# Attention and maxout layers fused on one core: the second key batch's q moved behind its phi, k and v, with a new hand order of all pieces

## The chip, the cores and the metric

The kernel runs on one core of one Trainium2 chip. The metric is the device time of one execution in microseconds (us). Before the change the median of three runs is 160.75 us (160.62 to 160.98).

## The reference

Eight batches, eight heads, 576 positions, head size 64, 32 memory slots. All inputs and the output are float32.

```python
# q, k, v: (8, 8, 576, 64); phi: (8, 8, 576, 32)
a = softmax(phi, axis=2)                        # over the positions
k_m = einsum('bhsm,bhsd->bhmd', a, k)
v_m = einsum('bhsm,bhsd->bhmd', a, v)
attn = softmax(q @ k_m.T / 8, axis=-1) @ v_m    # (8, 8, 576, 64)
x = attn.transpose(0, 2, 1, 3).reshape(4608, 512)
h = maximum(maximum(x @ w1, x @ w2), x @ w3)    # w: (512, 768)
out = h @ w_out                                 # (768, 512)
```

## The kernel before

Everything is cut into pieces, one letter each, and one long string of words writes the order out by hand: `B@2` is piece B of batch 2, a number behind the letter is a part of it, and a `!` (the argument `swap`) gives a part of the piece's work to the other of two engines. `issue` (L769) turns a word into a call. Each engine runs its own instructions strictly in the order of the words, and waits at the first one whose inputs or buffers aren't ready. A second string, `banks`, gives the PSUM bank of each accumulation, in the same order.

What a batch goes through, with the letters:

- **Loads**, issued from GpSimd's queue: `L0` phi, `L1` k, `L2` v, `L3` q (L93, L97, L97, L112); `J0` and `J1` are the two halves of q of batch 1. k, v and q are converted from float32 to bf16 by the DMA, phi stays float32. phi and q have two buffers each, k two, and the tile that holds packed k beside v (`kvr`) three. `Y` loads weights. These DMAs share one queue and land in the order of their issue.
- **Sums over positions**: `E` exponentiates phi on ScalarE. From batch 2 on, `r` copies k into `kvr` (on GpSimd, with `!` on ScalarE, L102), so that `B` (L247) gives the sums of k and v and the softmax denominator in one pass. Batches 0 and 1 do it in two: `B0` for k, `B1` for v. `N` (L269) divides by the denominator: a reciprocal on VectorE, and then the scaling, one instruction for v and two for k on VectorE, or with `!` two and two on ScalarE. `K` (L309) transposes the result and copies it out of PSUM (VectorE, with `!` ScalarE).
- **Scores**: `Q0`, `Q1` transpose q in blocks on VectorE (L323); `S` (L337) multiplies and exponentiates on ScalarE. `a`, `s`, `c`, `m`, `X` form the softmax of the scores on VectorE (`m` without `!` on GpSimd). `M`, `R`, `X` do it another way, with ScalarE, for three groups of batches 0 and 1.
- **Folded weights**: `D` multiplies v_m into the weights w1 - w3 and w2 - w3 (`D3`: into w3 times w_out), casts by ScalarE or VectorE. `V0` to `V3` (L213) subtract w3 from columns 0 to 511, 512 to 767, 1024 to 1535 and 768 to 1023 of w1 and w2, on VectorE or, with `!`, GpSimd. They overwrite the weights that the folds of batch 0 have read, and come before the folds of batch 1.
- **First layer**: `F0` to `F11` (L505), even ones followed by a relu on ScalarE (with `!` VectorE), odd ones by a maximum on VectorE.
- **Second layer**: for batches 0 and 1 `t` (L667) does the first four of six blocks and `T` (L680) the rest, or `T` does all; `g` sends a row block of batch 0 by ScalarE's queue. From batch 2 on it is done by a Strassen-like scheme of seven products `P` (L590), with sums `A` of activations and sums `U` of weights, on GpSimd or VectorE. `U0` to `U3` with @9 are the sums of w_out.

PSUM has eight banks; `B`, `D`, `F` and each half of `S` take two, the others one. A piece waits until the previous user of its banks has been copied out.

Of the kernel before, what the change touches and what calls it, by code (L numbers as in the profile page):

```python
# [15 lines left out]
def kernel(  # L16
# [14 lines left out]
    B, H, S, D = q.shape  # L31
# [32 lines left out]
    K1 = NP * NC * KS  # L64
# [73 lines left out]
    for i in range(P // M):  # L138
# [4 lines left out]
    banks = iter(  # L143
        "".join(
            """
            00232204420145545045026406426402640264023462467420742602462062460264024603604206
            42604620642164646240624607402604260240402402420724062042642024204204260424026427
            402742002442072420426045026520026265260602406243352
            """.split()
        )  # L150
    )
# [658 lines left out]
    for w in """  # L810
        E@0 h2@0 h3@0 h0@0 h1@0 L3@0 Z25@0 B0@0 Y2@0 I@0 N0@0 Z2@0 K0@0! Q0@0 Q1@0 Z9@0 S@0 Z2@0
        M0@0 M1@0 R0@0 R1@0 W0@0 Y3@0 W1@0 W2@0 Z6@0 O1@0 H3@0 O3@0 O2@0 H1@0 X1@0 B1@0
        X0@0 N1@0 K1@0 O0@0 Y0@0 D1@0! D0@0! D3@0 F10@0 F0@0! F8@0 Y1@0 L0@1 L1@1 J0@1
        F2@0! F6@0 V0@0! D4@0! D2@0 E@1 J1@1 F4@0! F1@0 F5@0 L2@1 F3@0 F7@0 F9@0 L3@2
        F11@0 B0@1 N0@1! t1@0 L1@2 t2@0 Q1@1 Q0@1 T2@0 K0@1! V1@0 V3@0 T1@0 S@1 L0@2
        B1@1 U0@9! N1@1! M1@1 a0@1 R1@1 t3@0 K1@1! T3@0 L2@2 s0@1 L1@3 c0@1 V2@0 D0@1
        D1@1! L0@3 D2@1 L2@3 t0@0 r0@2 X1@1 m0@1! X0@1 T0@0 F10@1! Q0@2 F6@1 E@2 F7@1
        F0@1 g2@0 F11@1 L3@3 F1@1 D3@1 Q1@2 F2@1 B@2 U1@9 F4@1 L1@4 L0@4 N@2 F3@1 F8@1
        K@2 g1@0 F5@1 L2@4 S@2 F9@1 D1@2! t3@1 E@3 D0@2 D2@2 D3@2 L3@4 a@2 T3@1 s@2 U3@9
        T4@1! c@2 m@2! r0@3 X@2 B@3 F0@2 U0@2 N@3 F8@2! F6@2 K@3 U1@2 Q0@3 L1@5 F2@2  # L820
        L0@5 Q1@3 U3@2 F10@2 g0@0 F3@2 F4@2 F9@2 F11@2 U2@9 S@3 a@3 s@3 t2@1 c@3 g3@0
        D3@3 D2@3 L2@5 U2@2 D0@3 U0@3 t0@1 r0@4! E@4 F1@2 T0@1! U1@3 F5@2 T2@1! F7@2
        t1@1 m@3 L3@5 A0@2! X@3 L0@6 T1@1! F6@3 F4@3! D1@3! B@4 N@4 L1@6 A1@2! F0@3 Q1@4
        F2@3 Q0@4 L2@6 A2@2! F8@3 K@4! F7@3 P1@2! F1@3 S@4 P2@2 F10@3 D0@4 a@4 D1@4!
        P0@2 A3@2! s@4 c@4 F3@3 P4@2 E@5 r0@5! F11@3 F9@3 m@4 F5@3 L3@6 P5@2 A0@3! T4@3!
        A1@3! D3@4 B@5 X@4 N@5 D2@4 Q1@5 Q0@5 P6@2 F2@4 K@5 P3@2 F10@4! S@5 L1@7 P1@3!
        D2@5 D1@5! a@5 F11@4 P2@3 F8@4 s@5 c@5 U2@3 L0@7 F4@4! F0@4 F6@4 r0@6! L2@7 P0@3
        F1@4 F7@4 F9@4 P4@3 E@6 A2@3! A3@3! F3@4 F5@4 P3@3 D0@5 m@5 L3@7 U3@3 D3@5 B@6
        A0@4! A1@4! X@5 N@6 P5@3 F6@5 F8@5! Q0@6 r0@7 F2@5 Q1@6 F10@5 K@6! F9@5 U0@5
        F4@5 F7@5 P6@3! S@6 E@7 F3@5 P1@4 a@6 F5@5 F11@5 P2@4 D0@6 U0@4 B@7 D3@6 U2@4  # L830
        N@7 s@6 P0@4 A2@4! F0@5 F1@5 Q1@7 K@7! U1@4 A3@4! P4@4 D1@6! A0@5! D1@7! c@6
        D2@7! m@6 P3@4! U3@4 P5@4! D0@7 D2@6 D3@7 U2@6 Q0@7 X@6 T4@5 S@7 A1@5! A3@5!
        P6@4! F10@6 a@7 F6@6 s@7 F4@6 F11@6 F0@6 F7@6 c@7 P1@5 P2@5 F2@6! U2@5 F5@6 F3@6
        P0@5 U1@5 F1@6 m@7 F8@6 A2@5! X@7 P4@5 P3@5 F4@7 U0@6 U1@6 F10@7 U3@5 F9@6 P5@5!
        F5@7 F8@7 A0@6! P1@6! A1@6! F2@7 F6@7 F0@7 P6@5! U0@7 F7@7 F3@7 F1@7 P2@6! F11@7
        F9@7 A0@7 P0@6 A2@6! A1@7 P4@6 A3@6 U3@6! P1@7 P2@7 A2@7 P5@6 P3@6 U2@7! U1@7
        P4@7 P0@7! A3@7 P6@6 U3@7! P5@7 P3@7! P6@7! T4@7!
    """.split():
        n, b = w.rstrip("!").split("@")
        issue(int(b), n, w.endswith("!"))  # L840
# [30 lines left out]
```

## Time and profile before

| | |
|---|---|
| median of three runs | 160.75 us (160.62 to 160.98) |
| the profiled execution | 160.76 us, of which the span of the profile is 159.0 us |
| granted TensorE clock | 0.999 of full speed |
| busy | TensorE 149.6 us (94%), VectorE 116.8, GpSimd 109.2, ScalarE 98.8 |
| moved by DMA | 31.78 MB, 200 GB/s on average |

The profiled execution lies 0.01 us from the median of the runs, so a sum that is made against its trace can be read against the median as it is; 1.76 us of it are outside the span. "Idle before" an instruction means that its engine stood still; a releaser is what it waited for. Most of the 42 warm-up matmuls of line 164 (11.8 us) fill the first 20 us, in which little has been loaded.

In the issue table, the time to landing of a load counts from its issue on GpSimd to the moment that its completion can be seen.

### The profile page before, as it was taken

What the parts mean: (1) busy time and instruction counts of PE and PEld (TensorE: products, weight loads), DVE (VectorE), ACT (ScalarE), POOL (GpSimd) and SP (SyncE); (2) the same over time, 40 slices, a digit from 0 to 9 for tenths busy, and PEclk for the clock granted to TensorE, in tenths of its full rate; (3) what the DMA queues carried; (4) which work ended last, traced back from release to release, by engine and by line L of the source; (5) the groups of instructions that cost most, each with busy time, mean ns of one, the idle gap of its engine ahead of it and who ended that gap; (6) DMA issues with size and microseconds to landing.
All of it is one profiled execution on the core that took longest, in us unless ns stands there. A gap on an engine that the chain in (4) does not pass through costs nothing.

```text
span 159.0 us, 5179 instructions
## 1 busy us (share of the span) xinstructions
PE 149.6 (94%) x2218; PEld 100.3 (63%) x2228; DVE 116.8 (73%) x203; ACT 98.8 (62%) x142; POOL 109.2 (69%) x101
## 2 busy tenths in 40 slices
PE   6987798999798999999999999999999999999992
PEld 2442443574456538556776768887774888888871
DVE  2022803698988899787989688999998895679871
ACT  3205335723888699799699878886788826424110
POOL 7961102995039948889999999799969997890000
PEclk9999999999999999999999999999999999999999
DMA  5999999999999999999999999999303500332554
GB/s 150 168 199 209 205 210 211 281 207 210 207 281 225 298 236 243 307 262 214 323 246 277 213 255 284 278 239 246 111 0 136 200 4 0 132 132 70 177 187 164
DMA packets 22934, 31.78 MB, mean 200 GB/s; under 512 B 1152, under 2 KB 18560, under 8 KB 22912
## 3 DMA queue, kind: packets, MB, share of 16 engines
q0 software_dynamic: 16128, 21.43, 70.2%
q1 hardware_dynamic: 6064, 8.85, 15.8%
q10 hardware_dynamic: 720, 1.18, 2.2%
q8 instruction: 17, 0.28, 0.7%
q14 instruction: 5, 0.04, 0.1%
HBM read 39.32 MB, written 9.44 MB: 307 GB/s over the span
## 4 chain that ended last, share of the span: by engine, by line
PE 72%; DMA 19%; POOL 5%; issue 1%; ACT 1%; POOLq 0%
PE psum L513 26%; PE psum L624 24%; DMA w_sb<-in_moe_w_dram 13%; DMA kvr<-in_v_dram 6%; PE psum L462 5%; PE psum L690 4%; PE psum L672 3%; PE psum L256 3%; PE psum L699 2%; PE psum L351 2%; POOL ko L97 1%; PE psum L708 1%; POOL qq L112 1%; POOL w_sb L119 1%; PE psum L753 1%
## 5 line engine op out<-in xcount | busy, mean ns | idle before, releaser
L513 PE MATMUL psum<-hx,wp 128*128 128x288 bf16 x384 | 53.7, 286 | 0.7 <-DVE wp L181 0.3
L513 PEld LDWEIGHTS <-wp 128*128 128x128 bf16 x384 | 36.6, 98 | 12.3 <-issue 1.5
L526 DVE TENSOR_TENSOR hx<-psum,h 128x576 bf16<-128x576 f32 x48 | 34.1, 744 | 3.3 <-PE psum L513 2.7
L177 ACT CAST wp<-psum 128x1024 bf16<-128x1024 f32 (+1 forms) x30 | 28.2, 993 | 2.7 <-PE psum L462 2.3
L175 ACT ACTIVATE h<-psum 128x576 bf16<-128x576 f32 x38 | 23.8, 651 | 8.9 <-PE psum L513 8.7
L624 PEld LDWEIGHTS <-hx 128*128 128x128 bf16 x192 | 18.4, 98 | 3.5 <-issue 0.9
L360 ACT ACTIVATE e<-psum 128x576 bf16<-128x576 f32 x16 | 9.5, 649 | 7.5 <-PE psum L351 7.5
L549 POOL TENSOR_TENSOR w_sb<-hx 128x1024 bf16<-128x1024 bf16 x5 | 10.6, 2130 | 4.0 <-DVE hx L526 2.6
L164 PE MATMUL psum<-warm 128*128 128x512 bf16 x42 | 11.8, 435 | 1.4 <-DVE warm L131 1.2
L330 DVE STREAM_TRANSPOSE qT<-qq 128x576 f32<-128x576 f32 x16 | 11.6, 757 | 2.0 <-DMA qq<-in_q_dram 2.0
L624 PEld LDWEIGHTS <-w_sb 128*128 128x128 bf16 x120 | 11.4, 98 | 2.5 <-issue 0.7
L107 POOL COPY kvr<-ko 128x2304 bf16<-128x2304 bf16 x3 | 6.3, 2108 | 7.7 <-DMA ko<-in_k_dram 7.7
L218 POOL TENSOR_TENSOR w_sb<-w_sb 128x2048 bf16<-128x2048 bf16 x1 | 4.1, 4065 | 10.4 <-PE psum L462 10.4
L436 POOL TENSOR_TENSOR t<-t,sm 128x1152 bf16<-128x1152 bf16 x5 | 10.6, 2127 | 0.6 <-DVE sm L429 0.5
L549 POOL TENSOR_TENSOR w_sb<-w_sb,hx 128x1024 bf16<-128x1024 bf16 x5 | 10.6, 2128 | 0.3
L234 ACT ACTIVATE e<-ph 128x1152 bf16<-128x1152 f32 (+1 forms) x9 | 9.6, 1063 | 1.8 <-DMA ph<-in_phi_dram 1.8
L549 POOL TENSOR_TENSOR hx<-hx 128x1024 bf16<-128x1024 bf16 x5 | 10.7, 2130 | 0.0
L549 POOL TENSOR_TENSOR twb<-wp 128x256 bf16<-128x256 bf16 x11 | 7.3, 670 | 3.9 <-ACT wp L177 3.9
L624 PE MATMUL psum<-w3T,hx 128*128 128x256 bf16 x72 | 9.8, 273 | 0.0
L624 PE MATMUL psum<-wo_sb,hx 128*128 128x256 bf16 x72 | 9.8, 273 | 0.0
L656 DVE TENSOR_TENSOR ot<-psum,snap 128x512 f32<-128x512 f32 x12 | 8.3, 689 | 1.9 <-PE psum L624 1.3
L97 POOL DMA_DIRECT2D ko<-in_k_dram x11 | 7.7, 700 | 2.9 <-DMA qq<-in_q_dram 1.5
(106 smaller groups left out, 272.2 us busy)
## 6 DMA issues: line engine op xcount, KB each, us to landing
out_dram<-ot SPq DMA_DIRECT2D x8, 512.0 KB, 4.2
qq<-in_q_dram POOLq DMA_DIRECT2D x7, 576.0 KB, 13.5
ph<-in_phi_dram POOLq DMA_DIRECT2D x7, 576.0 KB, 15.3
ko<-in_k_dram POOLq DMA_DIRECT2D x7, 576.0 KB, 16.1
kvr<-in_v_dram POOLq DMA_DIRECT2D x7, 576.0 KB, 18.0
out_dram<-ot SPq DMA_DIRECT2D x14, 256.0 KB, 2.2
w_sb<-in_moe_w_dram POOLq DMA_DIRECT2D x3, 768.0 KB, 17.9
out_dram<-ot ACTq DMA_DIRECT2D x4, 256.0 KB, 6.2
```

The costliest lines, as they stand in the source:

```text
L97: nc.gpsimd.dma_start(out=kv[:, h].rearrange("p j c d -> p j (c d)"), in_=by_pair((k, v)[i], b)[:, h],)
L164: nc.tensor.matmul(po[:, 0:BANK], lhsT=warm[:, 0:P], rhs=warm, start=True, stop=True)
L175: nc.scalar.activation(out=out_, in_=in_, func=AF.Relu)
L177: nc.scalar.copy(out=out_, in_=in_)
L234: nc.scalar.activation(out=s["e"][:, js], in_=loaded[b]["ph"][:, js], func=AF.Exp)
L330: nc.vector.transpose(out=s["qT"][:, j].rearrange("p j c r e -> p (j c r e)").bitcast(FP32), in_=loaded[b]["q"][:, j].rearrange("p j c d - ...
L360: nc.scalar.activation(out=e2[:, a].rearrange("p (t r c) -> p t r c", t=2, c=NC), in_=sc[a][:, :, 0:SH].rearrange("p t (c r) -> p t r c", ...
L436: (nc.vector if swap else nc.gpsimd).tensor_tensor(out=t, in0=t, in1=x.to_broadcast(list(t.shape)), op=ALU.mult,)
L513: nc.tensor.matmul(acc[:, h, 0:SH], lhsT=wps[b][:, g, w * DF + ft * P : w * DF + (ft + 1) * P], rhs=attn[:, g, c0 : c0 + SH], start=(g == ...
L526: nc.vector.tensor_tensor(out=hT[:, row(ft), (b % 2) * S : (b % 2 + 1) * S].rearrange("p (h n) -> p h n", h=2), in0=a, in1=s["h1", ft], op ...
L549: eng.tensor_tensor(out=out_, in0=in0, in1=in1, op=op)
L624: nc.tensor.matmul(po[:, q * CH : (q + 1) * CH], lhsT=lhs(k, q), rhs=rhs(k), start=(i < 3 and k == 0 and q == 0), stop=(k == KT and q == 1 ...
```

## The change

No piece is added or dropped: the same 382 words behind the common start stand in another order, some with `!` put on or taken off, and with other PSUM banks.

- q of batch 2 (`L3@2`) is issued behind phi, k and v of batch 2; before it came ahead of them. The order becomes phi, k, v, q.
- `r0@2` (the packing of k of batch 2 on GpSimd) now comes ahead of the four loads of batch 3.
- The block `t0@0` moves ahead of `B0@1`; `S@1` comes ahead of `T1@0`.
- Of the weight differences, `V1@0` goes to GpSimd and `V0@0` to VectorE (before the other way round), and `U0@9` goes from VectorE to GpSimd.
- `N` of batches 2 and 7 scales on ScalarE (batch 1 did already). `K` of batches 2 and 3 is copied out by ScalarE.
- Behind batch 3, order and engines of many first-layer and second-layer pieces differ. The last three words are the same.

```diff
     banks = iter(
...
-            00232204420145545045026406426402640264023462467420742602462062460264024603604206
...
+            00232204420145545045026402640240624602467406065460260246042064064204620465026406
...
-        X0@0 N1@0 K1@0 O0@0 Y0@0 D1@0! D0@0! D3@0 F10@0 F0@0! F8@0 Y1@0 L0@1 L1@1 J0@1
-        F2@0! F6@0 V0@0! D4@0! D2@0 E@1 J1@1 F4@0! F1@0 F5@0 L2@1 F3@0 F7@0 F9@0 L3@2
-        F11@0 B0@1 N0@1! t1@0 L1@2 t2@0 Q1@1 Q0@1 T2@0 K0@1! V1@0 V3@0 T1@0 S@1 L0@2
-        B1@1 U0@9! N1@1! M1@1 a0@1 R1@1 t3@0 K1@1! T3@0 L2@2 s0@1 L1@3 c0@1 V2@0 D0@1
-        D1@1! L0@3 D2@1 L2@3 t0@0 r0@2 X1@1 m0@1! X0@1 T0@0 F10@1! Q0@2 F6@1 E@2 F7@1
-        F0@1 g2@0 F11@1 L3@3 F1@1 D3@1 Q1@2 F2@1 B@2 U1@9 F4@1 L1@4 L0@4 N@2 F3@1 F8@1
-        K@2 g1@0 F5@1 L2@4 S@2 F9@1 D1@2! t3@1 E@3 D0@2 D2@2 D3@2 L3@4 a@2 T3@1 s@2 U3@9
-        T4@1! c@2 m@2! r0@3 X@2 B@3 F0@2 U0@2 N@3 F8@2! F6@2 K@3 U1@2 Q0@3 L1@5 F2@2
-        L0@5 Q1@3 U3@2 F10@2 g0@0 F3@2 F4@2 F9@2 F11@2 U2@9 S@3 a@3 s@3 t2@1 c@3 g3@0
...
+        X0@0 N1@0 K1@0 O0@0 Y0@0 D1@0! D0@0! D3@0 F8@0! F10@0! Y1@0 L0@1 L1@1 F0@0!
+        F4@0! F2@0 D2@0 D4@0! J0@1 F1@0 V1@0! F3@0 F6@0 J1@1 L2@1 L0@2 F7@0 L1@2 E@1
+        F11@0 F5@0 L2@2 L3@2 F9@0 t0@0 B0@1 N0@1! t2@0 T2@0! K0@1! Q0@1 t1@0 Q1@1 V2@0
+        U2@9 S@1 T1@0 V3@0 B1@1 U0@9 N1@1! V0@0 a0@1 M1@1 r0@2 R1@1 t3@0 K1@1! L1@3 s0@1
+        L0@3 c0@1 T0@0! D0@1 m0@1! X1@1 X0@1 D2@1! D1@1! T3@0! F4@1! F2@1! E@2 F5@1
+        F10@1 F3@1 F6@1 B@2 N@2! F7@1 F0@1 Q1@2 K@2! F8@1 Q0@2 F11@1 g1@0 g2@0 F9@1 L2@3
+        S@2 F1@1 a@2 L3@3 U1@9 L1@4 s@2 c@2 D3@1 D0@2 D3@2 D1@2! t3@1 U3@9 r0@3 E@3 m@2!
+        U0@2 D2@2 L0@4 T4@1! X@2 T3@1 F4@2! g3@0 B@3 F10@2 L2@4 N@3 U1@2 F2@2 L3@4 F11@2
+        K@3! U3@2 F0@2 F6@2 L1@5 U2@2 Q1@3 F8@2 g0@0 Q0@3 L0@5 F3@2 F9@2 S@3 t2@1 L2@5
...
-        N@7 s@6 P0@4 A2@4! F0@5 F1@5 Q1@7 K@7! U1@4 A3@4! P4@4 D1@6! A0@5! D1@7! c@6
...
+        A3@4! D0@6 B@7 N@7! D3@6 s@6 U3@4 P0@4! F3@5 Q0@7 A0@5! K@7! P4@4 D1@6! D1@7!
...
```

More of the change, by code (lines that the diff above doesn't have):

```diff
@@ L145 @@
             """
-            00232204420145545045026406426402640264023462467420742602462062460264024603604206
-            42604620642164646240624607402604260240402402420724062042642024204204260424026427
-            402742002442072420426045026520026265260602406243352
+            00232204420145545045026402640240624602467406065460260246042064064204620465026406
+            24026402460346406426046204620624126421426426442604206420647024204204042042064206
+            126412646226416246204260560650262626406246526567574
             """.split()
@@ L818 @@
-        F0@1 g2@0 F11@1 L3@3 F1@1 D3@1 Q1@2 F2@1 B@2 U1@9 F4@1 L1@4 L0@4 N@2 F3@1 F8@1
-        K@2 g1@0 F5@1 L2@4 S@2 F9@1 D1@2! t3@1 E@3 D0@2 D2@2 D3@2 L3@4 a@2 T3@1 s@2 U3@9
-        T4@1! c@2 m@2! r0@3 X@2 B@3 F0@2 U0@2 N@3 F8@2! F6@2 K@3 U1@2 Q0@3 L1@5 F2@2
-        L0@5 Q1@3 U3@2 F10@2 g0@0 F3@2 F4@2 F9@2 F11@2 U2@9 S@3 a@3 s@3 t2@1 c@3 g3@0
-        D3@3 D2@3 L2@5 U2@2 D0@3 U0@3 t0@1 r0@4! E@4 F1@2 T0@1! U1@3 F5@2 T2@1! F7@2
-        t1@1 m@3 L3@5 A0@2! X@3 L0@6 T1@1! F6@3 F4@3! D1@3! B@4 N@4 L1@6 A1@2! F0@3 Q1@4
@@ L824 @@
[L824 to L829, printed above, removed]
@@ L830 @@
-        F4@5 F7@5 P6@3! S@6 E@7 F3@5 P1@4 a@6 F5@5 F11@5 P2@4 D0@6 U0@4 B@7 D3@6 U2@4
-        N@7 s@6 P0@4 A2@4! F0@5 F1@5 Q1@7 K@7! U1@4 A3@4! P4@4 D1@6! A0@5! D1@7! c@6
[L832 to L835, printed above, removed]
@@ L836 @@
-        F9@7 A0@7 P0@6 A2@6! A1@7 P4@6 A3@6 U3@6! P1@7 P2@7 A2@7 P5@6 P3@6 U2@7! U1@7
-        P4@7 P0@7! A3@7 P6@6 U3@7! P5@7 P3@7! P6@7! T4@7!
+        X0@0 N1@0 K1@0 O0@0 Y0@0 D1@0! D0@0! D3@0 F8@0! F10@0! Y1@0 L0@1 L1@1 F0@0!
[3 more added lines that the diff above has]
+        L0@3 c0@1 T0@0! D0@1 m0@1! X1@1 X0@1 D2@1! D1@1! T3@0! F4@1! F2@1! E@2 F5@1
@@ new lines @@
+        F10@1 F3@1 F6@1 B@2 N@2! F7@1 F0@1 Q1@2 K@2! F8@1 Q0@2 F11@1 g1@0 g2@0 F9@1 L2@3
+        S@2 F1@1 a@2 L3@3 U1@9 L1@4 s@2 c@2 D3@1 D0@2 D3@2 D1@2! t3@1 U3@9 r0@3 E@3 m@2!
+        U0@2 D2@2 L0@4 T4@1! X@2 T3@1 F4@2! g3@0 B@3 F10@2 L2@4 N@3 U1@2 F2@2 L3@4 F11@2
+        K@3! U3@2 F0@2 F6@2 L1@5 U2@2 Q1@3 F8@2 g0@0 Q0@3 L0@5 F3@2 F9@2 S@3 t2@1 L2@5
+        D3@3 D2@3 r0@4! a@3 D0@3 s@3 t1@1 E@4 c@3 m@3 L3@5 F5@2 T2@1! F7@2 T1@1! X@3
+        t0@1 T0@1 F1@2 F0@3 D1@3! B@4 U0@3 F2@3 N@4 L0@6 F6@3 A0@2! F1@3 Q0@4 F10@3 L1@6
@@ new lines @@
+        A1@2! K@4! F8@3 Q1@4 F4@3 L2@6 F3@3 F9@3 P1@2 F11@3 S@4 A2@2! P2@2 A3@2! D1@4!
+        a@4 U2@3 D0@4 s@4 c@4 P4@2 F5@3 r0@5! F7@3 E@5 P0@2! P5@2! T4@3! m@4 D3@4 B@5
+        D2@4 A0@3! L3@6 L0@7 X@4 U1@3 L1@7 N@5 Q0@5 P6@2 A1@3! F2@4 Q1@5 F0@4 K@5 P3@2
+        S@5 F3@4 F10@4 F8@4 F6@4 a@5 F9@4 L2@7 U0@4 F4@4 s@5 L3@7 D2@5 D1@5! c@5 F7@4
+        P1@3! E@6 m@5 r0@6! A2@3! F11@4 P0@3 P2@3 F5@4 F1@4 X@5 P4@3 D0@5 U3@3 B@6 D3@5
+        N@6 P5@3 Q0@6 F8@5 Q1@6 F0@5 K@6! A3@3! A0@4! P6@3! U0@5 F1@5 E@7 S@6 P3@3 F6@5
@@ new lines @@
+        U1@4 F10@5 a@6 A2@4! F7@5 F11@5 F9@5 r0@7! F2@5! F4@5 P1@4 F5@5 A1@4! U2@4 P2@4
+        A3@4! D0@6 B@7 N@7! D3@6 s@6 U3@4 P0@4! F3@5 Q0@7 A0@5! K@7! P4@4 D1@6! D1@7!
+        c@6 U0@6 D2@7! P3@4 P5@4! D0@7 Q1@7 D3@7 D2@6! T4@5! m@6 X@6 S@7 a@7 P6@4 F0@6
+        F2@6 s@7 c@7 A1@5! F8@6 A2@5! F4@6 U1@5 P1@5 F9@6 F1@6 F6@6! P2@5! m@7 F10@6
+        P4@5! F7@6 X@7 U1@6 U2@5 F11@6 P0@5 A3@5! F5@6 F3@6 P5@5 F4@7 U3@5 P3@5 F2@7
+        F3@7 P6@5 F5@7 F0@7 A0@6! F8@7! F6@7! F10@7 F7@7 P1@6! F1@7 P2@6! F9@7 F11@7
@@ L838 @@
+        A1@6! U0@7! U3@6 A3@6 A0@7 P4@6 U2@6 P0@6 A2@6! U1@7! A1@7 P1@7 A2@7 P5@6 P3@6!
+        P2@7 U3@7! U2@7! P4@7 A3@7 P6@6! P0@7 P5@7 P3@7 P6@7! T4@7!
     """.split():
```

## The prediction

> **What bounds the kernel now.** I read the chain of waits first, then the timelines of TensorE and GpSimd from 20 to 66 us, the issue table window by window for each load's time to landing, and last the rest of TensorE's timeline. The chain of waits, with the start and length of each stretch:
>
> ```profile
> 8.77 21.28 DMA w_sb<-in_moe_w_dram
> 30.04 0.03 POOLq L93
> 30.07 0.87 issue
> 30.95 0.73 POOL qq L112
> 31.68 8.85 DMA kvr<-in_v_dram
> 40.53 0.04 issue
> 40.58 0.75 PE psum L256 x72
> ```
>
> Until 40.5 us the loads set the end; the last is v of batch 1, for which B1@1 (L256) waits. From there the chain is TensorE work to its last matmul at 155.9 us, and 3.1 us of copy and store follow. So the change can win only by work brought ahead of B1@1, or from the small waits behind it. TensorE's timeline shows these (in brackets the idle time):
>
> ```profile
> 28.17 2.13 PE L513 MATMUL psum<-hx,wp 128*128 128x288 bf16 x16 [0.30 <-DVE wp L181]
> ...
> 39.33 0.47 PE L351 MATMUL psum<-qT,kvt 32*32 32x288 bf16 x32
> 40.58 0.75 PE L256 MATMUL psum<-kvr,e 64*32 64x64 bf16 x72 [0.77 <-DMA kvr<-in_v_dram]
> ...
> 43.39 1.01 PE L462 MATMUL psum<-w_sb,kvt 64*32 64x512 bf16 x24
> ...
> 49.73 0.65 PE L513 MATMUL psum<-hx,wp 128*128 128x288 bf16 x4 [0.23 <-DVE hx L526]
> 50.59 0.80 PE L256 MATMUL psum<-kvr,e 64*32 64x130 bf16 x72 [0.21 <-ACT wp L177]
> ```
>
> 0.77 us stand ahead of B1@1. Behind it, up to B@2 (50.59), there are 0.23, 0.21, and 0.17 in the 24 matmuls of L462, which take 0.94 from start to start in the chain and 0.77 later: together 0.61. From 66 us on gaps are 0.05 at most. GpSimd, which issues the loads:
>
> ```profile
> 26.94 4.07 POOL L218 TENSOR_TENSOR w_sb<-w_sb 128x2048 bf16<-128x2048 bf16 x1 [10.39 <-PE psum L462]
> 30.95 0.74 POOL L112 DMA_DIRECT2D qq<-in_q_dram  x1
> 31.68 0.77 POOL L97 DMA_DIRECT2D kvr<-in_v_dram  x1
> ...
> 46.40 2.10 POOL L107 COPY kvr<-ko 128x2304 bf16<-128x2304 bf16 x1 [7.70 <-DMA ko<-in_k_dram]
> 48.45 0.74 POOL L112 DMA_DIRECT2D qq<-in_q_dram  x1
> ```
>
> Issue plus time to landing gives: k of batch 1 34.2, q halves 36.25 and 37.65, v 40.55; batch 2: q 43.45, k 46.3, phi 47.8, v 50.45; batch 3: k 54.05, phi 55.65, v 59.05. The stream has no hole, so a load costs the distance to the one before: q and k 2.9, phi 1.5, v 2.65. At 50.59, B@2's v had landed 0.14 earlier.
>
> **The change, part by part.** Prices of TensorE pieces are start to start: F 0.49, D 0.22 (the first after full-array work 0.34), t 0.87, T behind a t 0.86, B 0.74, S 0.41, and 0.11 for the change back to full-array work.
>
> *Up to B1@1.* F8 and F10 now run first and fill the 0.30 us before F0, which needs D0's cast (ends 28.11). VectorE then has from 28.11 four relus (0.70 each), D4's cast (1.16) and six maxima (0.70): the fourth maximum is done at 34.9, the sixth at 36.3 (before 36.87). TensorE gets to t0@0 at about 34.0 to 34.3 and waits for the fourth, until 34.9. Then t0 0.87, B0@1 0.74, t2 0.98, T2 0.86, K0 0.1, t1 0.87, S 0.41, T1 0.97: 40.7. S's inputs, Q0 and Q1, are done at 38.4 (the second half of q lands at 37.65, each transpose 0.71). v of batch 1 still lands at 40.55: what is ahead of it in the stream is unchanged. So B1@1 starts 0.12 later than before, with t0@0 and its switch (0.98) done: a lead of 0.85. Bounds: 0.3 if VectorE is 0.55 later at t0, 0.98 if TensorE is never late.
>
> *V1@0 on GpSimd for V0@0.* 128x1024 two-input work takes 2.13 there (L549), instead of 4.07. The next issues, the second half of q and v of batch 1, leave some 2 us earlier, and nothing is won: the stream is busy with k and q until 36.25. On VectorE V0@0 costs 1.16 (the 128x2048 row of L218), V2@0 1.16 as before, V3@0 0.64; placed behind Q1, the three run from 38.4 to 41.3, ahead of D0@1 at 43.6. Before, V2@0 ran at 42.77, which is the 0.17 in L462. U2@9 and U0@9 on GpSimd (1.65 each) end by 37, in time where GpSimd stood idle until 46.40: nothing.
>
> *From B1@1 to B@2.* B1, M1, t3, K1 and a T took 2.88 and do again: D0@1 at 43.6. Three D 0.78, T3 0.97, six F 2.94: B@2 at 48.3. Its inputs: phi first 42.1, k 45.0, packed by r0@2 at 47.05, v 47.7. VectorE behind V0 (41.3): a0 0.47, s0 0.78, c0 0.27, m0 0.73, X1 0.70, X0 0.44 is 44.7, ahead of F4@1 at 45.3; then D2's cast to 45.8, T3's copy, two relus to 47.8, each within 0.2 us of the matmuls that need its bank. I take 0.1 for these: B@2 at 48.4. The 0.61 of before is gone, the lead 1.35 (0.85 + 0.61 - 0.1).
>
> *From B@2 to F2@2: lost again.* N@2 goes from VectorE (0.21 + 0.52 behind the reciprocal) to ScalarE: four pieces, 0.52 (L282) and 0.63 (L305) a pair, 1.15. What queues behind it there: F0's relu 0.58, K's copy 0.46, F8's relu 0.58; then S@2's exponentials 1.14, casts of D3@1, D0@2, D3@2, D1@2 (0.94 each), E@3 1.07, D2@2's cast 0.94, copies of T4@1 and T3@1 1.06. From the reciprocal's end at 49.4 to 52.2 it runs through; S@2's exponentials wait for TensorE (52.4) and end at 53.8; the rest is 7.0: 60.6. F2@2 needs T3@1's bank. TensorE would come to it, from B@2 at 48.4 without any wait, at 59.8 (11.4 of pieces): 0.8 late by this engine. Two more limits fall in the same place. q of batch 2 is now last, at 50.45; Q1 and Q0 (1.42) end at 51.9, before S@2. Behind S@2 VectorE needs 4.65 (a 0.80, s 1.37, c 0.40, m 1.36, X 0.72): X@2 at 58.5, where F4@2 would start at 58.0. And B@3 needs v of batch 3, 59.05, where TensorE would be at 58.5. These three waits overlap, and cost their largest, 0.6 to 0.9 together; before had 0.15 in this stretch. Net 0.6: the lead falls from 1.35 to 0.75.
>
> *The g's.* g1, g2 and g3 issue stores from ScalarE, now inside that full stretch. The issues last 0.34 to 0.37, but at 48.23 one went beside a running E, with the next ScalarE instruction starting at 48.91, on time. I take nothing, at most 1.05 for three.
>
> *Loads of batch 3.* k, phi and v of batch 3 were issued at 36 to 38.7; behind r0@2 they go out at 47.05 to 49.3. q of batch 2 keeps the stream busy until 50.45, so the price is nil if a load starts within 3.4 us of its issue. No load in the trace shows that with an empty queue; the shortest landing, the 144 KB parts of k of batch 0, took 4.0 to 5.5. So 0 to about 1.4; I take 0, as the first load has 3.4 us.
>
> *Behind batch 3.* I went along the new order for each result's margin before its use. Behind F2@2 a shift of 0.6 leaves all of them positive; the narrowest is N@7 on ScalarE, 0.20 + 1.15 = 1.35 against the 1.69 of D3@6, P0@4 and F3@5 before K@7. Nothing there to win or lose. The last three words and the tail (3.1) are unchanged.
>
> Sum: 160.76 - 0.75 = 160.0, and the median stands 0.01 from that execution.
>
> [...] In the new order m@2 on VectorE (two SBUF inputs, from about 56.6) meets GpSimd's r0@3 (from k's landing at 54.05, to 56.15) closely; before, m@2 ran at 58.13 and GpSimd was idle. The trace has no such pair running at once. [...]
>
> **The rivals.**
>
> - *The late loss doesn't come* (ScalarE keeps up, v of batch 3 lands half a us early): the lead of 1.35 stays, 159.4. For: v and the q half of batch 1 are issued earlier. Against: the ScalarE sum. 0.15.
> - *ScalarE pays for the g's*: 1.05 on a queue that is already last: 161.0 at full price, 160.6 at half. Against: the issue at 48.23. 0.12.
> [...]
> - *Slower: the loads of batch 3 come late*, because they are issued 10 us later behind r0@2. Place: B@3. The lead is used up when v of batch 3 lands at 59.9 instead of 59.05, and each us after that is a us. For: v of batch 4 took 4.95 us of the stream (66.85 to 71.8) instead of 2.65, beside stores; the stream can stretch. At that price (+2.3) 162.2, at 1.4 161.3. Against: the 3.4 us of cover, and that only g1 and g2 go out before 59, as before. 0.16.
> - The change might also do nothing at B1@1, if t0 came 0.85 late. I count it with the first bound.
>
> **How the numbers follow.** My forecast, 160.0, has 0.50. A measurement can tell 0.2%, 0.3 us: faster is below 160.4, slower above 161.1. Faster: forecast 0.50, no late loss 0.15, half of m@2 0.03: 0.68. Slower: loads 0.16, ScalarE at its full price, which lies on the border, 0.04: 0.20. The rest, 0.12, is the same. The range goes from 159.3 (no late loss, and t0@0 never late: 0.98 for 0.85) to 161.1 (ScalarE at its full price), which leaves out most of the late loads.
>
> **What would show it.** Right: no idle time at B1@1, which starts at 40.6 to 40.8; B@2 near 48.4; N@2 on ScalarE 1.15 and ScalarE without gaps from 53 to 60; B@3 at 59.1 to 59.4; v of batch 3 landing near 59.05; TensorE's last matmul near 155.2. Wrong: v of batch 3 past 59.9, or a gap above 0.5 us on TensorE behind 66 us, or t0@0 starting behind 35.5.

## The result and the profile after

The changed kernel takes 162.05 us (median of 19 runs, 160.78 to 163.08); the kernel before, on the same chip, 160.64 (19 runs). The ratio is 1.0072, interval 1.0047 to 1.0096: slower by 0.7%, where 160.0 was forecast. Ratios leave out slow executions, of which there were two, both of e1 (below) at a granted clock of 0.979, its profiled one among them. The profiled execution took 161.32 (span 159.5, granted clock 0.997), 0.73 less than the median. A second profile of the same kernel (a1 below) took 162.73, so both are read here.

The chain of waits after, at the place where before it went through the load of v of batch 1:

```profile
5.78 14.26 DMA wo_sb<-in_moe_w_out_dram
20.09 4.05 PE psum L197 x18
...
31.77 3.60 PE psum L513 x28
46.09 2.94 PE psum L513 x24
51.22 1.28 DVE qT L330 x2
54.63 1.01 ACT wp L177
```

From 20.04 us on the chain holds no load any more, only work. But its last load is now `wo_sb`, the weights of the second layer, which set the start of the first fold (the `D` of batch 0, L462). TensorE's timeline (start, length, what, idle before):

```profile
26.70 0.30 PE L462 MATMUL psum<-w_sb,kvtn 64*32 64x256 bf16 x8
27.93 2.62 PE L513 MATMUL psum<-hx,wp 128*128 128x288 bf16 x20
...
31.77 3.60 PE L513 MATMUL psum<-hx,wp 128*128 128x288 bf16 x28 [0.27 <-ACT wp L177]
35.21 1.03 PE L672 MATMUL psum<-wo_sb,hx 128*128 128x512 bf16 x3
...
41.15 0.75 PE L256 MATMUL psum<-kvr,e 64*32 64x64 bf16 x72
43.96 1.15 PE L462 MATMUL psum<-w_sb,kvt 64*32 64x512 bf16 x24
...
48.95 0.81 PE L256 MATMUL psum<-kvr,e 64*32 64x130 bf16 x72
...
51.17 0.29 PE L315 MATMUL psum<-ident,kvn 128*128 128x128 bf16 x2 [0.27 <-ACT kvn L305]
...
55.68 1.02 PE L672 MATMUL psum<-wo_sb,hx 128*128 128x512 bf16 x3 [0.37 <-ACT wp L177]
...
60.38 0.81 PE L256 MATMUL psum<-kvr,e 64*32 64x130 bf16 x72
```

The waits of before at F0, B1@1 and B@2 are gone (no bracket in the rows at 27.93, 41.15 and 48.95). B@2 comes at 48.95 instead of 50.59. But at B@3 (60.38) the lead has turned into a delay of 0.8 us, though in this execution B@3 waits for nothing. GpSimd after:

```profile
44.96 2.10 POOL L107 COPY kvr<-ko 128x2304 bf16<-128x2304 bf16 x1 [7.91 <-DMA ko<-in_k_dram]
47.00 0.79 POOL L97 DMA_DIRECT2D ko<-in_k_dram  x1
47.78 0.76 POOL L93 DMA_DIRECT2D ph<-in_phi_dram  x1
48.52 0.75 POOL L97 DMA_DIRECT2D kvr<-in_v_dram  x1
```

These are the loads of batch 3, as foreseen at 47 to 49.3. What they did to the stream is seen in the DMA rate, one figure for each half microsecond from 44 to 64 us. Before:

```profile
GB/s 313 389 367 288 230 221 207 210 205 205 207 210 224 221 281 364 395 331 349 288 256 236 194 210 202 277 280 279 222 210 205 207 207 205 212 210 256 309 330 323
```

After:

```profile
GB/s 207 214 200 210 233 194 203 205 203 138 111 168 189 194 200 200 272 385 399 325 177 177 145 150 165 230 280 304 262 290 263 233 212 203 210 210 203 212 203 233
```

Before, no half microsecond is below 194. After, the rate has a hole, a stretch well below that, at 48.5 to 50 (138, 111, 168) and another at 54 to 56.5 (177, 177, 145, 150, 165). v of batch 3 lands at 60.02 instead of 59.06. In this execution that was just in time for B@3; in a1 it landed at 61.34, and B@3 waited.

### The profile page after: what moved, and what is told of

It reads as the page before. It is cut to its first block, busy times and chain, and to the rows that moved or that the text cites. A ratio compares the mean times of both kernels' runs of the same rounds, so it can differ in the third digit from the quotient of the medians.

```text
span 159.5 us, 5176 instructions
## 1 busy us (share of the span) xinstructions
PE 149.8 (94%) x2217; PEld 100.2 (63%) x2228; DVE 117.3 (73%) x197; ACT 100.6 (63%) x151; POOL 107.0 (67%) x100
## 4 chain that ended last, share of the span: by engine, by line
PE 79%; DMA 9%; ACT 3%; POOL 3%; DVE 3%; issue 2%; DVEq 0%; POOLq 0%
PE psum L513 28%; PE psum L624 23%; DMA wo_sb<-in_moe_w_out_dram 9%; PE psum L690 5%; PE psum L672 4%; PE psum L256 4%; PE psum L462 4%; PE psum L197 3%; PE psum L699 2%; DVE hx L526 2%; PE psum L351 2%; POOL ko L97 1%; ACT wp L177 1%; PE psum L708 1%; PE psum L753 1%
## 5 line engine op out<-in xcount | busy, mean ns | idle before, releaser
L513 PE MATMUL psum<-hx,wp 128*128 128x288 bf16 x384 | 53.0, 286 | 0.4 <-ACT wp L177 0.3
L175 ACT ACTIVATE h<-psum 128x576 bf16<-128x576 f32 x37 | 22.8, 661 | 12.0 <-PE psum L513 11.8
L177 ACT CAST wp<-psum 128x1024 bf16<-128x1024 f32 (+1 forms) x28 | 26.5, 990 | 2.0 <-PE psum L462 1.8
L436 POOL TENSOR_TENSOR t<-t,sm 128x1152 bf16<-128x1152 bf16 x5 | 10.6, 2126 | 5.5 <-DVE sm L429 5.4
L638 ACT COPY snap<-psum 128x512 f32<-128x512 f32 x9 | 5.3, 588 | 8.4 <-PE psum L624 8.3
L107 POOL COPY kvr<-ko 128x2304 bf16<-128x2304 bf16 x2 | 4.2, 2106 | 7.9 <-DMA ko<-in_k_dram 7.9
L112 POOL DMA_DIRECT2D qq<-in_q_dram x9 | 6.9, 770 | 3.7 <-DMA w_sb<-in_moe_w_dram 3.7
## 6 DMA issues: line engine op xcount, KB each, us to landing
ph<-in_phi_dram POOLq DMA_DIRECT2D x7, 576.0 KB, 13.5
```

Of the source, the lines that this page charges most:

```text
L175: nc.scalar.activation(out=out_, in_=in_, func=AF.Relu)
L177: nc.scalar.copy(out=out_, in_=in_)
L436: (nc.vector if swap else nc.gpsimd).tensor_tensor(out=t, in0=t, in1=x.to_broadcast(list(t.shape)), op=ALU.mult,)
L513: nc.tensor.matmul(acc[:, h, 0:SH], lhsT=wps[b][:, g, w * DF + ft * P : w * DF + (ft + 1) * P], rhs=attn[:, g, c0 : c0 + SH], start=(g == ...
```

## The experiments

Ratios are to the kernel before, run on the same chip, with 95% intervals. Times of single pieces are from one profile of each kernel.

**a1: the changed kernel, unedited.**

> The changed kernel again, unedited, for a second profile and more times. Theory 1 (late loads): k, phi and v of batch 3 are issued behind the packing of k of batch 2 and find the queue nearly empty; where the time is above the first profile's 161.3, v of batch 3 lands later than 60.0 and the matmuls B@3 start behind 60.4 by as much. Theory 2 (full engines): ScalarE and VectorE between B@2 and F4@2 set the time; F4@2 starts at 59.6 to 60 in each profile and the extra time stands elsewhere. Theory 3 (no slack in front): the start of the first fold (26.70 in the first profile, 25.97 before) and of B1@1 (41.15) move from run to run and the time follows by the same amount. Times 160.8 to 163.

161.69 us (10 runs, 160.73 to 162.92), ratio 1.0053 (1.0021 to 1.0085). TensorE's timeline of a1:

```profile
59.76 0.65 PE L513 MATMUL psum<-hx,wp 128*128 128x288 bf16 x4
61.43 0.80 PE L256 MATMUL psum<-kvr,e 64*32 64x130 bf16 x72 [1.02 <-POOL twb L549]
```

B@3 stood for 1.02 us. The releaser named, a sum of weights on GpSimd, is not an input of B: in the first profile that sum ran at 60.70, behind the start of B@3 (60.38). v of batch 3 landed at 61.34, 0.09 ahead of B@3, and is the one. That the longer executions are of this kind is likely, since b1 takes most of their spread away; a trace shows it for this one.

**b1: the four loads of batch 3 back ahead of r0@2, all else as changed.**

```diff
-  B1@1 U0@9 N1@1! V0@0 a0@1 M1@1 r0@2 R1@1 t3@0 K1@1! L1@3 s0@1 L0@3 c0@1 ... L2@3 ... L3@3
+  B1@1 U0@9 N1@1! V0@0 a0@1 M1@1 L1@3 L0@3 L2@3 L3@3 r0@2 R1@1 t3@0 K1@1! s0@1 c0@1 ...
```

> The changed kernel with the four loads of batch 3 issued ahead of r0@2 again (at 37 to 41 us instead of 47 to 50). Theory 1: v of batch 3 lands at 59.1 to 59.5, the time falls by 0.5 to 1.5 to 160.3 to 161, and its spread to about 0.3. Theory 2 and 3: no change beyond 0.2.

160.94 us (12 runs, 160.56 to 161.30), ratio 1.0009 (0.9997 to 1.0022): the loss is gone, and so is the spread, 0.74 us from the fastest to the slowest run instead of 2.2 and 2.3. v of batch 3 lands at 58.78, and the rate from 44 to 64 us has no slice below 196:

```profile
GB/s 203 214 207 233 196 198 207 207 203 214 207 203 217 212 300 369 329 314 270 251 205 207 248 292 294 279 284 276 230 209 205 212 205 207 210 200 233 305 314 366
```

The late loads cost 0.44 to 0.63% (from a1 and from the result), 0.7 to 1.0 us. But without them the changed order is only as fast as before.

**f1: the kernel before, with k, phi and v of batch 3 behind r0@2, and nothing else.**

```diff
-  L2@2 s0@1 L1@3 c0@1 V2@0 D0@1 D1@1! L0@3 D2@1 L2@3 t0@0 r0@2 X1@1
+  L2@2 s0@1 c0@1 V2@0 D0@1 D1@1! D2@1 t0@0 r0@2 L1@3 L0@3 L2@3 X1@1
```

> The kernel before with k, phi and v of batch 3 alone moved behind r0@2 (issued at 48.5 to 50.7 instead of 36 to 38.7). Theory 1: the rate of the loads falls below 190 GB/s for 1 to 2 us around 50, v of batch 3 lands 1 to 2 us late, B@3 waits for it, the time is 161.2 to 162.7 with a spread above 1. If a load needs less than 2 us from issue to its first byte, nothing changes: 160.7.

162.38 us (7 runs), ratio 1.0100 (1.0064 to 1.0136). The rate falls to 133, 81 and 88 GB/s from 49.5 to 51. v of batch 3 lands at 60.63, and TensorE waits for it by name:

```profile
59.05 0.62 PE L708 MATMUL psum<-wp,hx 128*64 128x512 bf16 x4
60.78 0.80 PE L256 MATMUL psum<-kvr,e 64*32 64x130 bf16 x72 [1.11 <-DMA kvr<-in_v_dram]
```

One part of the change alone makes the old order slower by 1.6 us.

**k1: the changed kernel with only k of batch 3 ahead of r0@2.**

```diff
-  a0@1 M1@1 r0@2 R1@1 t3@0 K1@1! L1@3 s0@1
+  a0@1 M1@1 L1@3 r0@2 R1@1 t3@0 K1@1! s0@1
```

> The changed kernel with one of the four loads of batch 3, k, moved back ahead of r0@2; phi, v and q of batch 3 stay behind. Theory of an empty queue (a load pays only where nothing else is queued behind the one in flight): k of batch 3 lands at 53.0 to 53.6, phi and v are issued 5 us ahead of that and follow without a hole (no half microsecond under 185 GB/s from 48 to 58), v lands at 58.8 to 59.3, and the time is within 0.3 us of that with all four loads ahead (160.9). Rival, each load needs its own issue some 8 us or more ahead: k lands as early, but a hole comes at 53 to 56 ahead of phi, v lands at 60 or later, and the time is 161.5 or more.

161.03 us (12 runs, 160.46 to 161.29), ratio 1.0024 (1.0012 to 1.0037). phi and v of batch 3 were issued about as late as in the changed kernel (46.58 and 47.32 instead of 47.78 and 48.52), yet with k in the queue (issued at 37.00) there is no hole, and v lands at 59.12:

```profile
GB/s 210 210 207 207 224 198 207 203 207 205 212 207 212 214 290 350 362 335 256 237 210 205 250 284 286 286 275 283 232 215 212 203 205 207 210 207 226 318 344 332
```

So a late issue as such is harmless where another load already stands in the queue; what costs is a late issue of the load next in line. In the changed kernel k of batch 3 was issued at 47.00, 3.5 us ahead of the landing of q of batch 2 (50.49), and the hole still opened at 48.5, while q was running out. The trace of the changed kernel doesn't show when k's first byte came, only that the rate stays below 195 until 51, 4 us behind the issue of k.

Two things stay open. In the hole the DMA engines don't stand still: from 48.5 to 50 they are shown as busy for 0.3 to 0.9 of each slice of 0.04 us, but with 191 packets, where k1 has 278; why a short queue slows them isn't shown. And the second hole opens when v and q of batch 3 and k of batch 4 have long been issued (48.52 to 51.61). It comes only in profiles that have the first one (a1, c1, d1 and f1, not b1 and k1), so it goes back to the late issue, but not to a queue about to run empty at that moment. Measured against 205 GB/s, the two holes lack about as much, 0.11 MB each, so each is worth some 0.5 us (an estimate from the rates above).

**g1: b1 with q of batch 2 first again (L3@2 ahead of L0@2).**

```diff
-  J1@1 L2@1 L0@2 F7@0 L1@2 E@1 F11@0 F5@0 L2@2 L3@2 F9@0
+  J1@1 L2@1 L3@2 L0@2 F7@0 L1@2 E@1 F11@0 F5@0 L2@2 F9@0
```

> The changed kernel with the loads of batch 3 early (as in b1) and q of batch 2 ahead of phi, k and v again. Theory 4: Q@2 is free of q's landing, but v of batch 2 lands 2.9 later, at 50.3, and B@2 starts at 50.4 instead of 48.6; what is ahead of B@2 in this order can't cover it: 161.5 to 163. If the order of the four loads matters little: 160.9 as b1.

162.78 us (6 runs), ratio 1.0124 (1.0090 to 1.0158). TensorE of g1 stands where the change was to help:

```profile
50.10 0.80 PE L256 MATMUL psum<-kvr,e 64*32 64x130 bf16 x72 [1.62 <-DMA kvr<-in_v_dram]
```

In this order the new sequence of the loads is worth 1.15%, 1.8 us. Its mechanism, v earlier for B@2, works.

**e1: the kernel before, with q of batch 2 moved behind v of batch 2, and nothing else.**

```diff
-  F5@0 L2@1 F3@0 F7@0 F9@0 L3@2 F11@0 ... K1@1! T3@0 L2@2 s0@1
+  F5@0 L2@1 F3@0 F7@0 F9@0 F11@0 ... K1@1! T3@0 L2@2 L3@2 s0@1
```

> The kernel before with q of batch 2 alone moved behind phi, k and v of batch 2. Theory 1 (late loads): the loads of batch 3 stay issued early, so the time stays within 0.2 of 160.7. Theory 4 (q behind costs by itself): q lands at 50.4 instead of 43.4, the transposes Q move behind it and S@2, at 53.67 before, starts 0.3 to 1 later; B@3 with it, if the chain from S@2 to F0@2 is the limit: 160.9 to 161.7.

165.03 us (median of all 6 runs), ratio 1.0221 (1.0175 to 1.0267): the slowest kernel here, though no load is late. k of batch 2 now lands at 43, and `r0@2`, its packing, moves to where VectorE works. GpSimd of e1:

```profile
43.11 2.31 POOL L107 COPY kvr<-ko 128x2304 bf16<-128x2304 bf16 x1 [4.88 <-DMA ko<-in_k_dram]
45.37 0.74 POOL L112 DMA_DIRECT2D qq<-in_q_dram  x1
46.12 1.64 POOL L549 TENSOR_TENSOR w3T<-wo_sb,w3T 128x768 bf16<-128x768 bf16 x1
```

VectorE of e1, X1@1 (L395) and m0@1 (L436), each with two inputs in SBUF:

```profile
43.38 2.65 DVE L395 TENSOR_TENSOR hx<-e,r 128x576 bf16<-128x576 bf16 x1
45.95 2.43 DVE L436 TENSOR_TENSOR t<-t,sm 128x576 bf16<-128x576 bf16 x1
```

They take 0.76 in the changed kernel. TensorE needs their result for F10@1, the next F in this order, stands for 3.05 us, and then runs at half its clock. The stretches of e1 (window, its length, busy times; the granted clock is the third figure from the end):

```profile
47.50:48.00 0.50, 0.00 (x0) 0.00 (x0) 0.50 (x1) 0.00 (x0) 0.50 (x2) 1.00 1.19 205
48.00:48.25 0.25, 0.00 (x0) 0.00 (x0) 0.25 (x1) 0.00 (x0) 0.25 (x1) 0.80 1.11 189
48.25:48.50 0.25, 0.00 (x0) 0.00 (x0) 0.21 (x2) 0.00 (x0) 0.24 (x1) 0.50 1.30 221
...
54.50:54.75 0.25, 0.25 (x2) 0.00 (x0) 0.21 (x1) 0.00 (x0) 0.06 (x1) 0.50 1.13 184
54.75:55.00 0.25, 0.25 (x9) 0.12 (x8) 0.02 (x1) 0.00 (x0) 0.00 (x0) 0.55 1.22 207
55.00:55.50 0.50, 0.50 (x11) 0.25 (x4) 0.50 (x1) 0.15 (x1) 0.00 (x0) 1.00 1.22 207
```

By the means of 0.80 and 0.55 the clock fell at 48.15, some 2.3 us into the pause (45.90 to 48.95), and came back at 54.98, 6.0 us after work had resumed; the 24 matmuls of F took 5.92 us, for 3.10 in the changed kernel. The half clock thus cost 2.8 us, nearly as much as the pause itself. It doesn't fall so far in every execution: the six took 163.34 us at a granted clock of 1.000, 164.64 to 165.20 at 0.987 to 0.990, and 165.95 (this one) and 166.09 at 0.979.

**i1: e1 with r0@2 on ScalarE.**

```diff
-  L2@3 t0@0 r0@2 X1@1 m0@1!
+  L2@3 t0@0 r0@2! X1@1 m0@1!
```

> The order before with only q of batch 2 moved behind v of batch 2 (that alone gave 165.0), and here also the packing of k of batch 2 (r0@2) on ScalarE instead of GpSimd. Shared port theory: alone, the earlier k put GpSimd's 2.3 us copy beside VectorE's X1@1 and m0@1, which took 2.65 and 2.43 instead of 0.75; TensorE stood for 3.05 us and then ran at half its clock for some 6 us. Without that copy on GpSimd the two take 0.75 again, TensorE's pause ahead of the F pieces stays under 1 us (the copy, some 2.1 us, now queues on ScalarE behind the casts and ahead of F6's relu and E@2), the granted clock stays at 1.00, and the time is 160.7 to 161.9. Load order theory (q at the end of batch 2's loads costs by itself, whatever VectorE does): the pause stays at 2 us or more and the time at 164 to 165.

163.09 us (4 runs), ratio 1.0155 (1.0135 to 1.0175). VectorE of i1:

```profile
42.13 1.81 DVE L218 TENSOR_TENSOR w_sb<-w_sb 128x2048 bf16<-128x2048 bf16 x1
43.87 0.74 DVE L395 TENSOR_TENSOR hx<-e,r 128x576 bf16<-128x576 bf16 x1
44.53 0.75 DVE L436 TENSOR_TENSOR t<-t,sm 128x576 bf16<-128x576 bf16 x1
```

Without a GpSimd instruction beside them both are back at 0.75, and the clock stays at 1.00; the one with 1.81 instead of 1.16 ran beside a sum on GpSimd (41.18 to 42.84). That shows what held VectorE. By its name the expectation's first theory takes the cause to be a port that the two share; no run shows a port, only these longer times. What it is worth in time is less: e1's one execution at full clock (163.34) is only 0.25 above i1's median, so by that execution i1 wins back the clock, but hardly the waits. The time lies between the two forecasts, because the copy, 2.15 us on ScalarE, now holds F's relus and E@2, and TensorE waits 1.01 and 1.06 for them. In the old order a q moved behind alone has no free engine for `r0@2`; the changed order has one, since it ends X1@1 and m0@1 at 44.54, 0.4 ahead of the copy at 44.96.

**c1: the changed kernel with N of batches 2 and 7 on VectorE again.**

```diff
-  B@2 N@2! F7@1 F0@1 ... B@7 N@7! D3@6
+  B@2 N@2 F7@1 F0@1 ... B@7 N@7 D3@6
```

> The changed kernel with the scaling of batches 2 and 7 back on VectorE. Theory 2: K@2 starts 0.3 earlier, S@2 and F4@2 by 0.3 to 0.5, the time falls by 0.3 to 0.5. Theory 1: B@3 still waits for v of batch 3, nothing beyond 0.2. Theory 3: nothing.

162.52 us (6 runs), ratio 1.0103 (1.0063 to 1.0143), not faster than a1. From B@2 to B@3 it took 11.54 us, against 11.43 in the changed kernel: scaling on ScalarE is not what was lost.

**d1: the changed kernel with r0@7 on GpSimd instead of ScalarE.**

```diff
-  F11@5 F9@5 r0@7! F2@5!
+  F11@5 F9@5 r0@7 F2@5!
```

> The changed kernel with the packing of k of batch 7 (r0@7) on GpSimd instead of ScalarE. In the first profile ScalarE is busy with it from 109.5 to 111.6, the relu behind it is late, and B@7 starts 0.35 later than the pieces ahead of it ended. If that wait counts, the time falls by 0.3 to 0.4; if k of batch 7 lands late in the slower runs, ScalarE waits there with all behind it, and the spread falls too. Theories 1 to 3: nothing beyond 0.2.

161.83 us (12 runs), ratio 1.0070 (1.0044 to 1.0097): no difference to a1 that the spread would show. The traces settle it: from S@6 to B@7 it took 7.55 us in d1 and 7.54 in the changed kernel, so this copy ahead of B@7 costs nothing.

**p0: the kernel before, unedited.**

> The kernel before, unedited, for a second profile. If the start of the first fold moves from run to run here too (25.97 in the first profile) while B@2 and B@3 stay at 50.6 and 59.6, the wait of 0.77 at B1@1 takes the difference up. If B@2 and B@3 move with it, the front's jitter is no difference of the two kernels. Time 160.5 to 160.9; no stretch under 190 GB/s between 44 and 64 us.

160.73 us (10 runs), ratio 0.9990 (0.9970 to 1.0010). Its use came from its trace. `wo_sb` landed at 19.89 instead of 19.28, the first fold began at 26.51 instead of 25.97, and B@2 started at 50.59, as before. ScalarE and TensorE of p0 there:

```profile
49.93 1.01 ACT L177 CAST wp<-psum 128x1024 bf16<-128x1024 f32 x1
50.59 0.81 PE L256 MATMUL psum<-kvr,e 64*32 64x130 bf16 x72
```

The profile of before names this cast as the releaser of B@2. Here B@2 began while the cast was still running, so B@2 doesn't need it; what B@2 waited for before is v of batch 2, which landed at 50.43.

**m1 and m2: three warm-up matmuls ahead of the first fold, in the kernel before (m1) and in b1 (m2).**

```diff
-  X0@0 N1@0 K1@0 O0@0 Y0@0 D1@0! D0@0! D3@0
+  X0@0 N1@0 K1@0 O0@0 Y0@0 Z3@0 D1@0! D0@0! D3@0
```

> The kernel before with three warm-up matmuls (128x512, 0.21 to 0.23 us each) added right ahead of the first fold D1@0, so that the front comes some 0.65 us later. Theory of the cushion (before, the start of B@2 is set by the landing of v of batch 2 at 50.4 us, not by the work ahead of it): the first fold starts 0.6 to 0.7 later, the wait ahead of B1@1 (0.77) and those up to B@2 shrink by as much, B@2 stays at 50.5 to 50.7, and the time stays within 0.2 us of the kernel before. Rival, the work ahead of it counts in full: B@2 at 51.1 or later, and 0.5 to 0.65 us more.

> The same three matmuls in the changed order with the loads of batch 3 ahead of r0@2 (which ran at 160.94 without them). Theory of the cushion: here nothing waits for a load between the first fold and B@2, so B@2 is 22.2 to 22.3 us behind the first fold as without them, and the time is 0.5 to 0.65 us longer, 161.4 to 161.6. Rival, some slack is left in this order too: B@2 less than 22 us behind the first fold, and less than 0.3 us more (up to 161.2).

m1: 161.23 us (12 runs), ratio 1.0027 (1.0012 to 1.0041). m2: 161.40 us (11 runs), ratio 1.0051 (1.0030 to 1.0072), which is 0.42% or 0.67 us above b1. A cushion here is a wait for a load that takes up delays of the work ahead of it. m2 came as the theory of the cushion had it. m1 lost 0.43 us, more than that theory's 0.2 and less than the rival's 0.5 to 0.65. Starts in us (the last stretch is the last 12 matmuls, L753):

```
                 before    p0     m1   | after     a1     b1     l1     m2
wo_sb lands       19.28  19.89  19.49  | 20.08  19.99  19.70  19.79  19.48
first fold        25.97  26.51  26.83  | 26.70  26.66  26.36  26.48  26.76
B@2               50.59  50.59  50.91  | 48.95  48.91  48.62  48.73  48.99
  since the fold  24.62  24.08  24.08  | 22.25  22.25  22.26  22.25  22.23
B@3               59.57  59.58  59.89  | 60.38  61.43  60.05  60.17  60.43
last stretch     154.41 154.41 155.04  | 155.00 156.40 154.63 154.52 155.09
```

Unedited, the first fold starts 6.6 to 6.7 us behind `wo_sb`, whose landing moves by 0.9 us from run to run (19.2 to 20.1 over the profiles). Before, B@2 waits for v of batch 2 at 50.4 whenever the fold starts ahead of about 26.5 (50.59 less 24.08); a front that is up to 0.54 late costs nothing, the rest counts in full. In the changed order B@2 is 22.25 behind the fold, always: the whole delay is passed on. In m1 the fold came 0.86 later, of which 0.32 reached B@2, as this has it; another 0.3 us was lost in S@3's own matmuls (0.82 instead of 0.48).

**l1: b1 up to S@3, from there the order, engines and banks of before.**

```diff
-  ... F3@2 F9@2 S@3 t2@1 L2@5 D3@3 D2@3 r0@4! a@3 D0@3 s@3 t1@1 E@4 ...   (changed order to the end)
+  ... F3@2 F9@2 S@3 a@3 s@3 t2@1 c@3 D3@3 D2@3 L2@5 D0@3 U0@3 t0@1 ...    (order of before to the end)
```

> The changed order up to S@3, with the loads of batch 3 ahead of r0@2, and from there on the order, engines and banks of the kernel before (bank numbers renamed so that they fit). Both orders have done the same TensorE pieces at S@3. Theory that the new order gives back 0.25 us behind batch 4: from the first fold (D1@0) to the start of the last stretch 127.95 to 128.1 us instead of 128.27, median 160.5 to 160.8. Theory that there is nothing to be had behind S@3: 128.2 to 128.3 and 160.9, as with the changed order throughout.

160.83 us (12 runs), ratio 1.0013 (0.9999 to 1.0027). From the first fold to the last stretch 128.04 us, 0.23 less than b1 (128.27) and 0.4 less than before (128.44). That is the first forecast, by one trace of each; the median is just above it and not told from b1's. No kernel here beat the one before.

## Why the prediction was wrong

*The step that failed: "Loads of batch 3".* It put the price at "0 to about 1.4; I take 0, as the first load has 3.4 us". The hole in the DMA rate, b1 and f1 show 0.7 to 1.0 us in the changed order and 1.6 in the old one. The mechanism stood there as the slower rival, with its place (B@3) and its sign (v of batch 3 past 59.9: it was 60.02 and 61.34), at a chance of 0.16. Its argument against, the cover of 3.4 us, failed: no row showed a load that begins behind a queue about to run empty, and the value was taken from the end that suited the sum. The next best row, the shortest landing on GpSimd's queue (4.0 to 5.5), already spoke for a late start. The rival's time, 161.3 to 162.2, holds the median. The last matmul ended at 156.5, where 155.2 was forecast.

That step is about half of the miss. Without the late loads (b1) the kernel takes 0.26 us more than before, where 0.75 less was forecast: a miss of 1.0 us, though still inside the range. The late loads add 0.7 to 1.0. In the first profile they cost nothing yet: from the first fold to B@3 it took 33.68 us, as in b1 (33.69). The other half is in the steps below.

*Up to B1@1.* Right in kind: no idle time at B1@1, t0@0 hidden. The wait forecast for t0@0 didn't come (the row at 35.21 has no bracket); one of 0.27 for a cast came at 31.77. From the first fold to B1@1 it took 14.45 where the steps (40.7 less 25.97) gave 14.73, 0.28 better. "v of batch 1 still lands at 40.55" held in the first profile (40.54), but this landing moves from run to run in both orders (39.75 in d1, 39.83 in f1). And 40.7 was counted from the fold of one profile. It fell at 25.8 to 26.7, and once no load was waited for, that entered the time in full; before, 0.54 of it did not. The prediction named this wait for v only as time to be won, and not as a cushion that the change removes.

*B1@1 to B@2.* 7.80 us for a forecast 7.7: right in sum. But not all of the 0.61 of waits went: the three D took 1.09 us for a price of 0.78, because the last of them waits for a copy on ScalarE (in the chain of waits from 44.07 to 44.66). The 0.1 that was taken for such waits and a T3 of 0.87 for 0.97 cover most of it. V1@0 on GpSimd cost nothing, as said.

*B@2 to F2@2: "lost again", 0.6.* Under-sized. From B@2 to F2@2 it took 12.65 (b1, whose loads were in time) instead of 12.2. ScalarE's walk was right: scaling 0.52 and 0.62, its last copy done at 61.32 for 60.6 plus the 0.55 by which B@2 was late. (The prediction's "rest" adds up to 6.8, not 7.0; its 60.6 goes by 6.8.) TensorE's own sum was wrong: pieces of 11.4 measured 12.0. T4@1, for which it shows no price, takes 1.96; F1@1 to the folds took 0.78 for a price of 0.49, of which the change of tile size is 0.1 (54.08 to 54.67 before, the same change without a wait) and the rest isn't explained. The waits, 0.27 for N@2's scaling and 0.37 for the first cast, came in the middle, not at F2@2.

*The g's.* Nothing, as taken: two were issued from 51.99 on beside a relu that starts at 51.99.

*Behind batch 3.* "Nothing there to win or lose" did not hold: by one trace of each, l1 got 0.23 us back with the old order. (The last three pieces are the same in both kernels, but P3@7 lost its `!`; the tail is 3.1 as before.)

*m@2 beside r0@3.* The 0.03 that the chances give to "half of m@2" is for a hold of m@2 by r0@3, which no run shows: r0@3 was done before m@2 began (54.01 to 56.12, m@2 at 57.33), and m@2 took 1.36, as before. What e1 shows is a GpSimd copy beside X1@1 and a sum of weights beside m0@1, with VectorE's times up from 0.76 to 2.65 and 2.43. In the changed kernel a sum of weights did run beside m@2, and there GpSimd's was the longer one: 1.67, for 0.68 of a sum of the same size at 60.36 in b1.

The sum of b1 closes by these terms: -0.75 forecast, +0.39 for its later fold, +0.23 behind S@3, and from the fold to B@3 33.69 instead of 33.3 (59.25 less 25.97), +0.4: together +0.27. The trace has +0.22 (154.63 against 154.41), the medians +0.26. The late loads come on top.

## What to carry to other kernels

A queue of loads should hold the next load well before the one in flight runs out. Here an issue 3.5 us ahead of the landing of the last load queued was too late, and one 13.5 us ahead (k1) was early enough; the limit between was not measured. Cost a load by when it is issued relative to the last one queued, and where no row shows a start behind a queue that runs out, take the upper end of its price. A wait for a load is also a cushion for everything ahead of it; when a change removes the wait, the spread of the earlier work becomes part of the time, so count from the mean of that start and not from one profile. When a load lands earlier, ask which copy on GpSimd starts with it, and what VectorE does in that stretch.

## What the runs showed of the hardware

- A GpSimd copy of 2.3 us held a VectorE instruction with two SBUF inputs for nearly its whole length: 2.65 instead of 0.76 us (e1), and 0.74 when the copy was on ScalarE (i1).
- A pause of TensorE of 3.05 us cost more than itself, some 2.8 us on top: the granted clock fell to 0.50 at 48.15, before the pause was over, and stayed there until 54.98, through 6.0 us of dense work (e1). From fall to return it is 6.83 us; what sets this length no run shows. Waits of 1.01 and 1.06 us left the clock at 1.00 (i1).
- A stall without a wait on data: behind S@3 one of four matmuls of t2@1 started 0.92 us late in d1 and 0.20 late in a1, and not in the first profile of the changed kernel, nor in before, b1 or c1. The row of d1 on TensorE:

```profile
66.80 0.60 PE L672 MATMUL psum<-wo_sb,hx 128*128 128x512 bf16 x2 [0.92 <-issue]
```

Around there each trace has a packet of an instruction queue (q8). In d1 and a1 it started between 64.5 and 65.5 us, in before, b1 and c1 between 62.5 and 63.0, in the first profile of the changed kernel between 63.5 and 64.0. Whether the late start goes back to that packet wasn't tried, and stays open. The late start may be part of the spread of the runs.
